# Fixed places on TensorE for the last inverse rows of a convolution, and another order of the first two gates' loads

## The chip, the cores and the metric

One core of a Trainium2 chip. The metric is device time in microseconds (us) of one launch of the whole program; lower is better. The kernel is the forward and backward pass of one layer in a single launch.

## The reference

The layer joins a long convolution (H3 style) with a bilinear gated unit; the kernel returns the output and the gradients of nine inputs. With B = 1, S = 2048, D = 1024, F = 3584, all in bf16:

```python
def ref_A(q, k, v, shift_k, ssm_k, ssm_D):
    k_shift = sum(k_pad[:, t:t + S, :] * shift_k[:, ks - 1 - t] for t in range(ks))
    kv = k_shift * v
    y = irfft(rfft(kv, 2 * S) * rfft(ssm_k, 2 * S))[:S]      # along S, per channel
    return q * (y + kv * ssm_D)

def ref_B(x, w_gate, w_up, w_down):
    h = (x @ w_gate) * (x @ w_up)
    return h @ w_down

xn = layernorm(x)
s = ref_A(xn, k, v, shift_k, ssm_k, ssm_D)
g = silu(ref_B(xn, w_gate, w_up, w_down))
out = x + s * g
# returned: out, and the gradients of x, k, v, shift_k, ssm_k, ssm_D, w_gate, w_up, w_down
```

## The kernel before

**Stages.** The 2048 rows are 16 blocks of 128 rows, the 1024 channels 8 slices of 128. First come the gate and up products (L645, 14 slabs of 256 columns), with the forward convolution running beside them on VectorE. Then come the down products `h @ w_down` (L969), taken as 8 pairs of blocks; each block has 28 chunks `fc` of 128 rows of `w_down`, and each chunk two halves of 512 columns, so a block has 56 matmuls and a pair 112. Behind each block stands a gate (`gate`, L1198): silu, its derivative, the output, and the gradients that go on. The weight gradients, the backward convolution and the last products with the layer norm's gradient follow.

**The forward convolution** is a transform along the rows, done per channel slice: short matmuls with cosine tables, and sums and differences on VectorE between them. It is a generator, `conv_forward` (L686), that yields after each piece a weight in us. `make_pump` (L465) gives two handles: `pump(frac)` takes pieces until the weights add up to that share of `F_TOTAL`, and `drain()` takes all that are left. `tick()` calls `pump` after each group of products, in the first pair after each odd chunk, so that the convolution's pieces are traced among the products.

**The last inverse.** For the last slice `inv8` (L395) leaves 16 segments of 256 values in the tile HX (called G in the code). `tail` (L744) then makes four row pairs: `inv8_rows` (L433) runs four matmuls for a pair (two rows, two segments each) into psY, a pool with a single buffer, and ScalarE copies psY into the tile yf (L750). After the fourth the tile goes to DRAM as YFd on GpSimd's queue. Row r reads the segments 2r and 2r + 1. The additions write the segments 0, 1, 4, 5, 8, 9, 12 and 13; the last four instructions of `inv8` (L283) write the pairs (2, 15), (10, 7), (14, 3) and (6, 11) in this order.

**The first pair.** Its down products are `bm_first` (L973): for a chunk, two matmuls for block 0 and two for block 1. Their PSUM is `ps_bm`, two buffers; blocks 2, 5, 8 and so on use `ps_bx`, one buffer. `bm_first(range(fc_, NF))` at L1260 traces all chunks that are left, then `drain()` at L1261 the rest of the convolution, so that the four row pairs are traced behind the first pair's products and ahead of block 2's. Then the gates of blocks 0 and 1 are traced, each with four loads on SyncE's queue: x, the output's gradient do, xn, and its rows of y, yf, which it reads back from YFd. After that the pairs 1 to 7 follow.

**Who sets the order.** The program isn't run as traced. A scheduler puts the instructions of each engine in an order, by trace order and by when it reckons that the inputs are there. Two marks bind it: `tc.keep_in_program_order(ins)` keeps the marked instructions in trace order among themselves (VectorE's, while `PIN[0]` is set, as it is through the forward convolution), and `with tc.issue_after(ins):` queues what is traced inside, on the engine of `ins`, behind `ins`. On the chip each engine works its own list in order, and so does each DMA queue.

## Time and profile before

| | |
|---|---|
| median of 3 runs | 1925.8 us (1925.4 to 1925.92) |
| the profiled execution: time, span | 1923.68 us, 1921.9 us |
| TensorE busy, matmuls | 1909.1 us (99%), 10946 |
| VectorE busy | 1554.5 us (81%) |
| ScalarE busy, GpSimd busy | 638.8 us (33%), 330.9 us (17%) |
| granted TensorE clock | 1.000 |
| first pair's down products | 511.8 to 537.0 us |
| the last four row pairs on TensorE | 537.0 to 545.7 us |
| store of yf issued, first load of yf issued | 546.8 us, 552.2 us |
| VectorE's first instruction that reads yf | 555.1 us |

Times inside the profile count from the start of the span, in us. A line of the order of time has the start, the length, the engine, the source line and operation, the tile written and the tiles read, and the count of merged instructions; in brackets the idle time of that engine before it, and what ended it. Matmuls overlap, so that one of 512 columns has a length of 0.379 us while the next starts 0.216 us after it. DVE is VectorE, ACT ScalarE, POOL GpSimd, SP SyncE, PE TensorE; SPq is SyncE's DMA queue.

### The profile page before, as it was taken

To read this page: it belongs to the slowest core of one execution; us is meant where nothing else is said; L and a number is where in the kernel's file an instruction comes from. 1 tells how busy PE (TensorE), PEld (TensorE's weight loads), DVE (VectorE), ACT (ScalarE), POOL (GpSimd) and SP (SyncE) were. 2 spreads that over 40 slices of the span, in tenths; PEclk is the share of its full clock that TensorE was granted. 3 is DMA by queue.
4 is the path that set the end of the run, shared out by engine and by line. 5 is a ranking of instruction groups with operands and counts; after the bars stand their busy time and mean duration, and the time that the engine had idled before them with its cause. 6 is when DMAs were issued, how large, how long until landed. Compare 5 with 4: busy or idle time off the path is not lost.

```text
span 1921.9 us, 27410 instructions
## 1 busy us (share of the span) xinstructions
PE 1909.1 (99%) x10946; PEld 1028.1 (53%) x10946; DVE 1554.5 (81%) x1715; ACT 638.8 (33%) x943; POOL 330.9 (17%) x461
## 2 busy tenths in 40 slices
PE   8999999999999999999999999999999999999999
PEld 5555655555544456666666666664444444444444
DVE  8999999999967555887899999999996403388785
ACT  5754655545432233332222322221212102011113
POOL 5121212201112220001022131121212101011111
PEclk9999999999999999999999999999999999999999
DMA  8786867668799988657788688585796999889885
GB/s 296 266 262 217 261 208 236 219 219 279 262 272 326 304 296 249 205 190 240 244 256 269 214 261 261 196 273 174 230 251 174 154 204 215 157 184 186 176 174 188
DMA packets 451375, 444.41 MB, mean 231 GB/s; under 512 B 268816, under 2 KB 371628, under 8 KB 436784
## 3 DMA queue, kind: packets, MB, share of 16 engines
q1 hardware_dynamic: 394864, 243.36, 48.2%
q0 software_dynamic: 40064, 169.95, 27.7%
q10 hardware_dynamic: 16320, 29.36, 4.2%
q8 instruction: 85, 1.39, 0.3%
q14 instruction: 42, 0.34, 0.1%
HBM read 194.00 MB, written 185.64 MB: 198 GB/s over the span
## 4 chain that ended last, share of the span: by engine, by line
PE 71%; issue 17%; DVE 6%; POOL 3%; DMA 3%; ACT 1%; SPq 0%; POOLq 0%; DVEq 0%; ACTq 0%
PE psx L1472 20%; PE psb L1342 20%; PE psb L1420 9%; PE psb L1325 9%; PE psg L645 8%; PE psF L235 2%; DVE W L213 1%; DMA A<-DYd 1%; POOL Hd L66 1%; PE psY L1128 1%; PE psY L438 1%; PE psx L1420 1%; DVE HX L213 1%; DVE KX L213 1%; DMA yf_t<-YFd 1%
## 5 line engine op out<-in xcount | busy, mean ns | idle before, releaser
L645 PE MATMUL psg<-wslab,U 128*128 128x512 bf16 x1792 | 407.7, 379 | 2.9 <-DMA wslab<-in_B_w_gate_dram 2.0
L1342 PE MATMUL psb<-U,U 128*128 128x512 bf16 x1792 | 397.1, 379 | 0.0
L1472 PE MATMUL psx<-U,dgut 128*128 128x512 bf16 x1536 | 332.8, 379 | 0.0
L1472 PEld LDWEIGHTS <-dgut 128*128 128x128 bf16 x1792 | 175.3, 98 | 211.4
L1342 PEld LDWEIGHTS <-U 128*128 128x128 bf16 x1792 | 175.3, 98 | 197.9
L645 PEld LDWEIGHTS <-U 128*128 128x128 bf16 x1792 | 172.5, 98 | 187.5 <-issue 2.6
L1325 PE MATMUL psb<-wdt,U 128*128 128x256 bf16 x1792 | 205.6, 273 | 0.0
L1325 PEld LDWEIGHTS <-U 128*128 128x128 bf16 x1792 | 175.2, 98 | 29.2
L213 DVE TENSOR_TENSOR W<-W 128x1024 f32<-128x1024 f32 (+1 forms) x186 | 183.9, 1005 | 3.9
L1420 PE MATMUL psb<-U,U 128*128 128x512 bf16 x816 | 177.1, 379 | 0.0
L1347 ACT CAST wb<-psb 128x512 bf16<-128x512 f32 x112 | 65.6, 586 | 315.4 <-PE psb L1342 304.4
L969 PE MATMUL psbm<-U,ht 128*128 128x512 bf16 x672 | 145.7, 379 | 0.0
L1420 PEld LDWEIGHTS <-U 128*128 128x128 bf16 x896 | 87.5, 98 | 104.5
L647 ACT CAST gut<-psg 128x512 bf16<-128x512 f32 x156 | 91.5, 588 | 123.6 <-PE psg L645 122.8
L1504 ACT ACTIVATE dx_t<-dxn 128x1024 bf16<-128x1024 f32 x15 | 15.9, 1057 | 319.4 <-DVE dxn L213 319.4
L1180 DVE SCALAR_TENSOR_TENSOR dkp<-dkT,kT 128x1024 bf16<-128x1024 bf16 (+2 forms) x64 | 78.3, 1224 | 37.6 <-DMA dkT<-DKSHd 35.9
L969 PEld LDWEIGHTS <-ht 128*128 128x128 bf16 x672 | 65.6, 98 | 78.6
L213 DVE TENSOR_TENSOR U<-U,dht 128x2048 bf16<-128x2048 bf16 x56 | 68.3, 1221 | 47.1 <-ACT dht L1327 47.1
L1327 ACT CAST dht<-psb 128x512 bf16<-128x512 f32 x112 | 65.7, 587 | 116.3 <-PE psb L1325 116.3
L66 POOL DMA_DIRECT2D Hd<-hN x54 | 37.0, 686 | 280.2 <-DVE hN L213 278.0
L213 DVE TENSOR_TENSOR dxn<-psx,dxna_t 128x1024 f32<-128x1024 f32 x15 | 18.3, 1222 | 76.5 <-PE psx L1472 70.7
L1451 ACT CAST wbs<-psb 128x512 bf16<-128x512 f32 x51 | 29.9, 586 | 145.3 <-PE psb L1420 137.2
(237 smaller groups left out, 2447.5 us busy)
## 6 DMA issues: line engine op xcount, KB each, us to landing
U<-GUd SPq DMA_DIRECT2D x28, 1024.0 KB, 7.5
DGd<-U SPq DMA_DIRECT2D x28, 1024.0 KB, 5.9
GUd<-gut ACTq DMA_DIRECT2D x39, 512.0 KB, 6.5
out_dram<-wb SPq DMA_DIRECT2D x112, 128.0 KB, 4.0
U<-Hd SPq DMA_DIRECT2D x14, 1024.0 KB, 6.0
Hd<-hN POOLq DMA_DIRECT2D x54, 256.0 KB, 4.7
HTd<-hT SPq DMA_DIRECT2D x52, 256.0 KB, 3.9
ht<-HTd SPq DMA_DIRECT2D x6, 1536.0 KB, 10.5
```

The source lines that it names most:

```text
L66: ins = nc.gpsimd.dma_start(out=out, in_=in_)
L213: pinned(V.tensor_tensor(o, a, b, op))
L645: gu_mm[0] = nc.tensor.matmul(ps[:], XNT[q][:, dc, qi * P:(qi + 1) * P], w[:, dc].rearrange("p a f -> p (a f)"), start=(dc == 0), stop=(dc ...
L647: nc.scalar.copy(out=gut[:, :, i], in_=ps[:].rearrange("p (a f) -> p a f", a=2))
L969: mm = nc.tensor.matmul(ps[:, dh * 512:(dh + 1) * 512], ht(fc)[:, i * P:(i + 1) * P], WD[fc // 4][:, fc % 4, dh * 512:(dh + 1) * 512], sta ...
L1180: ins = V.scalar_tensor_tensor(prod[:].rearrange("p r d -> p (r d)")[:, lo:H], dkT[:, 0, lo:H], 1.0, kT[:, 0, 13 + m + lo:13 + m + H], op0 ...
L1325: nc.tensor.matmul(ps[:, x * SLW:(x + 1) * SLW], DBMT[2 * hf + g][:, dc, (b % 4) * P:(b % 4 + 1) * P], wdt[:, dc, :], start=(dc == 0), sto ...
L1327: nc.scalar.copy(out=dht[:, 2 * e:2 * e + 2].rearrange("p b f -> p (b f)"), in_=ps[:])
L1342: nc.tensor.matmul(ps[:], XN[b // 4][:, b % 4, dc * P:(dc + 1) * P], dgus[b // 8][:, :, b % 8], start=(b == 0), stop=(b == NB - 1))
L1347: nc.scalar.copy(out=wb[:, dc % 2].rearrange("p a f -> p (a f)"), in_=ps[:])
L1420: nc.tensor.matmul(ps, h[:, f, b, :], DBM[b // 4][:, b % 4, dh * 512:(dh + 1) * 512], start=(b == 0), stop=(b == NB - 1))
L1472: nc.tensor.matmul(ps[:, dh * 512:(dh + 1) * 512], t[n][:, f, i * P:(i + 1) * P], WGU[n][:, f, dh * 512:(dh + 1) * 512], start=(n == 0 and ...
```

## The change

It has two parts.

The generator's piece ahead of the last four row pairs yields 1e6 in place of 3.0, so that `pump` stops there, and a third handle, `step()`, takes exactly one piece. The first pair's products are traced up to chunk 22, `pump(1.0)` traces what is left of the convolution up to that stop, and then each `step()` traces one row pair. Each row pair is queued behind the products traced just before it, and the products after it are queued behind its last matmul: chunk 23, row pair 0, chunks 24 and 25, row pair 1, chunks 26 and 27, row pair 2, chunks 0 to 2 of block 2, row pair 3, the other chunks of block 2.

The loads of a gate become a function of their own, `gate_rows`. For blocks 0 and 1 the loads of x, do and xn of both are traced first, then the loads of yf of both, and they are no longer queued behind the last weight load.

```diff
+    inv_mm = [None]
+
     def inv8_rows(G, psp, rp):
...
-                nc.tensor.matmul(ps[:, i, :], TI[:, 0, r, k, :], G[:, 2 * r + k, :], start=(k == 0), stop=(k == 1))
+                inv_mm[0] = nc.tensor.matmul(ps[:, i, :], TI[:, 0, r, k, :], G[:, 2 * r + k, :], start=(k == 0), stop=(k == 1))
...
+        def step():
+            next(gen, None)
+
...
-        yield 3.0
+        yield 1e6
         for _ in tl:
             yield 1.0
...
+    rows_in = {}
+
+    def gate_rows(b, first=0, last=None):
+        c, r = divmod(b, 8)
+        ins = []
+        for nm_, src in (("x_t", xq[:, c, r, :]), ("do_t", gout[:, c, r, :]), ("xn_t", xnn[:, c, r, :]), ("yf_t", YFd[:, b, :]))[first:last]:
+            t = mi.tile([P, D], BF16, name=nm_)
+            ld(t[:], src)
+            ins.append(t[:])
+        return ins
+
     def gate(b, ps):
         c, r = divmod(b, 8)
-        ins = []
-        for nm_, src in (("x_t", xq[:, c, r, :]), ("do_t", gout[:, c, r, :]), ("xn_t", xnn[:, c, r, :]), ("yf_t", YFd[:, b, :])):
-            t = mi.tile([P, D], BF16, name=nm_)
-            with tc.issue_after(wd_ld.ins) if b < 2 else nullcontext():
-                ld(t[:], src)
-            ins.append(t[:])
+        ins = rows_in.pop(b) if b in rows_in else gate_rows(b)
...
-    bm_first(range(fc_, NF))
+    bm_first(range(fc_, 23))
+    pump(1.0)
+    for fcs in ((23,), (24, 25), (26, 27)):
+        with tc.issue_after(inv_mm[0].ins):
+            mm = bm_first(fcs)
+        with tc.issue_after(mm.ins):
+            step()
+    ps2 = ps_bx.tile([P, D], F32, name="psbm")
+    with tc.issue_after(inv_mm[0].ins):
+        for fc in range(3):
+            mm = bm_mm(ps2, ht1[0], 0, fc)
+    with tc.issue_after(mm.ins):
+        step()
     drain()
...
+    for i in range(2):
+        rows_in[i] = gate_rows(i, 0, -1)
+    for i in range(2):
+        rows_in[i] += gate_rows(i, -1)
     for i in range(2):
         gate(i, pss[i])
...
-            ps = (ps_bx if (2 * bp + i) % 3 == 2 else ps_bm).tile([P, D], F32, name="psbm")
-            for fc in range(NF):
-                bm_mm(ps, ht, i, fc)
+            first = 2 * bp + i == 2
+            ps = ps2 if first else (ps_bx if (2 * bp + i) % 3 == 2 else ps_bm).tile([P, D], F32, name="psbm")
+            for fc in range(3 if first else 0, NF):
+                with tc.issue_after(inv_mm[0].ins) if first else nullcontext():
+                    bm_mm(ps, ht, i, fc)
```

More of the change, by code (lines that the diff above doesn't have):

```diff
@@ L481, in drain @@
             return n
-        return pump, drain
+        return pump, drain, step
     def staggered(main, tail, lag):
@@ L914, in build_kernel @@
     ps_cv = pool("ps_cv", 2, space=PSUM)
-    pump, drain = make_pump(conv, F_TOTAL)
+    pump, drain, step = make_pump(conv, F_TOTAL)
     cnt = [-5]
@@ L1190, in build_kernel @@
     C_TOTAL = 11.0 + 8 * FWD8_W + 16 * (PROD_W + INV8_W) + 8 * 1.4 + 8 * 2.5
-    bpump, bdrain = make_pump(conv_backward(), C_TOTAL)
+    bpump, bdrain, _ = make_pump(conv_backward(), C_TOTAL)
     ddo = const.tile([P, 8], BF16, name="ddo")
@@ L1465, in build_kernel @@
     PIN[0] = True
-    kpump, kdrain = make_pump(dk_units(kw_), DK_TOTAL)
+    kpump, kdrain, _ = make_pump(dk_units(kw_), DK_TOTAL)
     kcnt = [0]
```

## The prediction

> **What bounds the kernel now.** I read the waits of TensorE first, then the busy times by stretch, then the order of time on TensorE and VectorE around the edited place. TensorE is busy for 1909.1 of 1921.9 us. After the first 40 us it waits once for another engine; the columns are the total in us, the number of times and the longest:

> ```profile
> PE psY L438 <- DVE HX L283: 2.5, 1, 2.5
> ```

> That is the second row of the last inverse transform (TensorE at L438) waiting for VectorE. The stretches around it (length, then busy us of TensorE, its weight loads, VectorE, ScalarE, GpSimd, each with a count, then granted clock, DMA share and GB/s):

> ```profile
> 300.00:537.00 237.00, 236.60 (x1431) 129.18 (x1429) 234.63 (x227) 123.97 (x175) 34.23 (x48) 1.00 0.75 247
> 537.00:546.00 9.00, 6.46 (x38) 3.56 (x37) 5.18 (x8) 1.82 (x4) 0.00 (x0) 1.00 0.69 165
> ...
> 760.00:1300.00 540.00, 540.00 (x3421) 331.88 (x3420) 492.46 (x484) 155.99 (x260) 87.04 (x115) 1.00 0.74 238
> ```

> Two things matter. From 300 to 537 us VectorE is busy 99% of the time, so the moment at which it ends the last inverse is fixed by its own work. And from 546 us on TensorE has next to no gap (213.88 of 214.00, then 540.00 of 540.00), so whatever TensorE loses at the edited place nothing later gives back. Here is TensorE's order of time (start, length, line, operation, count, and the idle time before it):

> ```profile
> 517.38 19.80 PE L969 MATMUL psbm<-U,U 128*128 128x512 bf16 x91
> 537.02 0.38 PE L438 MATMUL psY<-HX,TI 128*128 128x256 bf16 x2
> 537.24 0.81 PE L969 MATMUL psbm<-U,U 128*128 128x512 bf16 x3
> 540.52 0.27 PE L438 MATMUL psY<-HX,TI 128*128 128x256 bf16 x1 [2.47 <-DVE HX L283]
> 540.63 1.02 PE L969 MATMUL psbm<-U,U 128*128 128x512 bf16 x4
> 541.73 0.27 PE L438 MATMUL psY<-HX,TI 128*128 128x256 bf16 x1
> 541.84 1.02 PE L969 MATMUL psbm<-U,U 128*128 128x512 bf16 x4
> ...
> 545.30 0.60 PE L438 MATMUL psY<-HX,TI 128*128 128x256 bf16 x4
> ```

> And VectorE's:

> ```profile
> 531.08 2.49 DVE L213 TENSOR_TENSOR HX<-W 128x512 bf16<-128x512 f32 x4
> 533.61 2.29 DVE L213 TENSOR_TENSOR W<-KX 128x2048 f32<-128x2048 bf16 x1
> 535.93 3.81 DVE L213 TENSOR_TENSOR W<-W 128x1024 f32<-128x1024 f32 x4
> 539.78 2.50 DVE L283 SCALAR_TENSOR_TENSOR HX<-W 128x512 bf16<-128x512 f32 x4
> 549.84 0.69 DVE L213 TENSOR_TENSOR gg<-bm,sig 128x1024 bf16<-128x1024 bf16 x1 [7.56 <-ACT sig L1212]
> ```

> The product loop gives 112 products to the first pair (28 chunks, 2 blocks, 2 halves). The trace has 16 from 511.78, 5 from 515.68 and these 91, so the first pair's last product stands right before 537.02. Spacing: (537.02 - 517.38) / 91 = 0.216 us. The products from 537.24 on belong to block 2. Row pair 0 of the inverse is rows 0 and 1: row 0 reads segments 0 and 1 of HX, written by the additions of 531.08; row 1 reads segments 2 and 3, and these come from the first and the third of the four instructions of 539.78, which the matmuls of 540.52 and 541.73 follow at once.

> **The change part by part.** (1) *Fixed places.* The new order is: chunk 23, row pair 0, chunks 24 and 25, row pair 1, chunks 26 and 27, row pair 2, three chunks of block 2, row pair 3, the rest of block 2. Each step is queued behind the last, so TensorE can't pull products past a row that isn't ready. Adding up the weights of the forward convolution, all of VectorE's work is traced when the planned stop comes (416.8 of 422.0), so each step does release one row pair. Row pair 0 thus moves 16 products ahead of where it stands now: chunk 23 ends at 517.38 + 75 x 0.216 = 533.6 us. Its first row goes at once (2 x 0.11 us, to 533.8), its second waits for VectorE. That engine has no gap in which to be earlier, and nothing of it is removed, so the matmuls come at 540.52 and 541.73 as now. At 541.84 TensorE has 96 products behind it; now it has 112 + 4 + 4 = 120 (one of the four after 537.24 is missing from the records). It is 24 products behind: **24 x 0.216 = 5.2 us**. Seen by gaps: 6.7 us idle in place of 2.5, and no four products between 540.63 and 541.73. After that no row waits: row pair 1 stands 8 products (1.7 us) later, at 543.6, and needs row pair 0's copy out of the single buffer, which ends at 542.6 (ScalarE, 0.59 us from 542.03), and segments from 539.78, the last done at 542.3. The next two have 1.7 and 1.3 us of products as their cover; without it each would cost about 0.9 us (0.3 to the copy's start, 0.59 for it).

> (2) *The clock after the gap.* A gap of 6.7 us, with one matmul and another 1.1 us behind it, is not in the trace before. The nearest rows are on both sides. The gap of 2.47 us is followed by products at full speed: four in 1.02 us, (1.02 - 0.38) / 3 = 0.21 us apart. The start of the program, where TensorE comes from rest, is not:

> ```profile
> 1.42 6.00 PE L521 MATMUL tr<-ident 128*128 128x128 bf16 x58 [1.42 <-POOL ident masks.py:199]
> 7.26 0.61 PE L586 MATMUL tr<-ident,x 128*128 128x128 bf16 x8
> ```

> 58 small matmuls take 5.84 us to the next, 0.101 us each; the eight after them start 0.056 us apart (7.26 to 7.71). The slow start cost 58 x 0.045 = 2.6 us. So the price is between 0 and 2.6 us, and no gain is possible since the products run at full speed now. I take **2.6 us**, since 6.7 us is nearly three times the gap that was harmless. The granted clock reads 1.00 at the start too, so that column won't tell. [...]

> (3) *Rows of the gates.* The eight loads of the first two gates stay on SyncE's queue, in another order: x, do and xn of both blocks, then both yf. Now the first yf holds the queue until the store of yf has landed, with the second block's four behind it:

> ```profile
> 547.09 0.33 SPq L61 DMA_DIRECT2D xn_t<-XNd  x1
> 552.24 0.33 SPq L61 DMA_DIRECT2D yf_t<-YFd  x1
> 552.62 0.43 SPq L61 DMA_DIRECT2D x_t<-in_A_q_dram  x1
> ```

> Six loads of about 0.4 us now fit into that wait, so the second block's come 4 us earlier. Worth for the end: nothing. VectorE works without a gap from 555.08 to 566.85 and so reaches the second gate when the first is through. TensorE needs from the gates only free PSUM: block 3 starts at about 553.5 and its buffer is copied out by 547.4; block 5 starts at about 578 and its buffer by 562.4. That cover of 6 and 16 us grows, since TensorE is later. The dropped ordering behind the last weight load (SyncE, 524.90) has no effect: these loads wait for the room of HX, and the first goes at 545.93, right behind the last row.

> (4) *What is late next.* Row pair 3 ends at 547.9 instead of 545.7, or 550.5 with the slow clock, so the store of yf and the gates come 2 to 5 us later: less than TensorE's own delay, so they set nothing.

> **Sum.** 5.2 + 2.6 = 7.8 us on the profiled execution's own 1923.7 us (span 1921.9 and 1.8 around it): 1931.5. The median of the runs is 2.1 us above that execution, so on it: 1925.8 + 7.8 = **1933.6 us**.

> **The rivals.**
> A, the forecast: 6.7 us gap and a slow restart, 1933.6. Chance 0.66.
> B, the gap without the slow restart: 1925.8 + 5.2 = 1931.0. For it: the 2.47 us gap did no harm. Against it: the start did. 0.15.
> C, not slower: the last four instructions of 539.78 are through by 533.6, because all of VectorE's work is now traced ahead of chunk 23. Then both waits vanish, 2.5 us and the 0.35 us of weight-load gaps, and the time is 1925.8 - 2.8 = 1923.0. It decides from the point where VectorE ends 8 us earlier; a VectorE without gaps since 300 us speaks against it. 0.08.
> D, the change doesn't do what it says: the rows are released later than their places (a step that spends itself on a piece of the transform), and end where they are now: 1925.8. The sum of weights speaks against it. 0.03.
> E, a second wait further on: all that follows is placed anew, and VectorE is 91% busy from 760 to 1300, so one row or product could come to wait as long as this one did: 1933.6 + 2.5 = 1936.1. For it only that tightness; against it, not one such wait now. 0.08.

> **Numbers.** A's own range is 1931.8 to 1935.2. The range of 8 in 10 takes in B below and ends short of E above: **1930.4 to 1936.0**. It leaves out C, D and most of E. A measurement here can't tell less than 0.2%, 3.9 us, from no change. A, B and E are beyond it, slower: 0.89. C and D are within it: 0.10. Faster by over 3.9 us would need more idle time than TensorE has at this place: 0.01.

> **What would show it.** The wait of L438 for HX at 6.7 us in place of 2.5, beginning near 533.8; 16 products after it before row pair 2; the products from 541.8 about 0.4 us apart for some microseconds (A) or 0.216 (B); rows 1 to 3 without a wait; the second gate's x, do and xn issued ahead of yf; TensorE without a gap thereafter. I am wrong if VectorE ends HX before 539, if products of block 2 stand ahead of row pair 0, or if TensorE gains a gap after 560.

## The result and the profile after

The changed kernel takes 1932.97 us (median of 8 runs, 1930.67 to 1941.11), the kernel before on the same chip 1925.53 us (8 runs, 1924.04 to 1927.16). The ratio is 1.0045, with a 95% interval of 1.0029 to 1.0062: slower by 7.4 us in the medians. The profiled execution took 1941.11 us, its span is 1939.3 us: the longest of the eight, and it has a second loss that the other profile of this kernel doesn't have, as the experiments show.

The waits of TensorE in the kernel after, past the first 20 us (total in us, times, longest):

```profile
PE psY L440 <- DVE HX L283: 7.4, 2, 6.6
PE psx L1501 <- DMA dgut<-DGd: 6.9, 2, 3.8
```

The first is the wait of before, tripled. The second is new and lies 1100 us later. TensorE's order of time at the edited place:

```profile
517.12 16.14 PE L974 MATMUL psbm<-U,U 128*128 128x512 bf16 x73
533.31 0.38 PE L440 MATMUL psY<-HX,TI 128*128 128x256 bf16 x2
540.28 0.37 PE L440 MATMUL psY<-HX,TI 128*128 128x256 bf16 x1 [6.59 <-DVE HX L283]
541.48 0.37 PE L440 MATMUL psY<-HX,TI 128*128 128x256 bf16 x1 [0.83 <-DVE HX L283]
541.65 3.62 PE L974 MATMUL psbm<-U,U 128*128 128x512 bf16 x8
545.06 1.06 PE L440 MATMUL psY<-HX,TI 128*128 128x256 bf16 x4
545.91 2.17 PE L974 MATMUL psbm<-U,U 128*128 128x512 bf16 x8
...
549.65 0.60 PE L440 MATMUL psY<-HX,TI 128*128 128x256 bf16 x4
550.09 23.04 PE L974 MATMUL psbm<-U,U 128*128 128x512 bf16 x104
```

Row pair 0 now comes 16 products earlier, and its second row waits until VectorE has written the segments that it reads: it starts at 540.28, against 540.52 before. The eight products from 541.65 take 3.41 us to the next line, 0.43 us each; the eight from 545.91 take 2.01, all but the first two at 0.22. The products ran at half pace for about five microseconds. VectorE's last inverse has not moved; only the first gate behind it comes 4 us later:

```profile
535.69 3.81 DVE L213 TENSOR_TENSOR W<-W 128x1024 f32<-128x1024 f32 x4
539.53 2.50 DVE L283 SCALAR_TENSOR_TENSOR HX<-W 128x512 bf16<-128x512 f32 x4
554.19 0.69 DVE L213 TENSOR_TENSOR gg<-bm,sig 128x1024 bf16<-128x1024 bf16 x1 [12.16 <-ACT sig L1223]
```

The stretches (length, busy us of TensorE, its weight loads, VectorE, ScalarE, GpSimd, then granted clock, DMA share, GB/s) show the half pace as a clock of 0.70 over 17 us, and no loss from 760 to 1300 us:

```profile
533.00:550.00 17.00, 9.53 (x40) 4.43 (x39) 8.86 (x10) 1.75 (x3) 0.00 (x0) 0.70 0.80 193
...
760.00:1300.00 540.00, 539.94 (x3443) 334.03 (x3442) 492.39 (x487) 159.88 (x264) 86.81 (x115) 1.00 0.73 235
...
1520.00:1910.00 390.00, 381.27 (x1726) 172.54 (x1760) 221.30 (x314) 50.67 (x72) 54.80 (x91) 0.99 0.94 190
```

In stretches of a quarter of a microsecond the clock reads 0.50 from 536.24 to 546.47 us, 10.24 us in all: it was halved while TensorE still waited, 2.5 us after its last matmul had ended (533.69), and stayed so for 6.2 us behind the wait.

On SyncE's queue the second gate's loads (551.82 to 552.76) do stand ahead of both loads of yf:

```profile
551.82 0.42 SPq L61 DMA_DIRECT2D x_t<-in_A_q_dram  x1
...
558.44 0.91 SPq L61 DMA_DIRECT2D yf_t<-YFd  x2
```

For comparing executions, call the **place time** the span from the last product of chunk 23 until the first pair, 20 products of block 2 and the four row pairs are through. Its work is 36 x 0.216 + 16 x 0.109 = 9.5 us. Before it was 545.74 - 533.57 = 12.2 us; after, with 14 more products added at 0.216 us since the rows end with 6: 550.09 + 3.02 - 533.31 = 19.8 us.

### The profile page after: what moved, and what is told of

It is laid out like the page before. It is cut to its first block, busy times and chain, and to the rows that moved or that the text cites. A ratio compares the mean times of both kernels' runs of the same rounds, so it can differ in the third digit from the quotient of the medians.

```text
span 1939.3 us, 27276 instructions
## 1 busy us (share of the span) xinstructions
PE 1907.9 (98%) x10812; PEld 1029.3 (53%) x10946; DVE 1554.3 (80%) x1715; ACT 638.5 (33%) x943; POOL 329.7 (17%) x461
## 4 chain that ended last, share of the span: by engine, by line
PE 83%; DVE 8%; DMA 4%; issue 2%; ACT 2%; SPq 1%; DVEq 0%; POOL 0%; ACTq 0%; POOLq 0%
PE psb L1371 20%; PE psg L650 18%; PE psb L1354 10%; PE psx L1501 9%; PE psb L1449 9%; PE psbm L974 9%; PE psF L235 3%; DVE dkp L1185 2%; DMA dkT<-DKSHd 2%; PE tr L679 1%; PE psY L440 1%; DMA dgut<-DGd 1%; DVE dxn L213 1%; DVE W L213 1%; PE psY L1133 1%
## 5 line engine op out<-in xcount | busy, mean ns | idle before, releaser
L650 PE MATMUL psg<-wslab,U 128*128 128x512 bf16 x1734 | 401.8, 379 | 5.2 <-DMA wslab<-in_B_w_gate_dram 1.1
L213 DVE TENSOR_TENSOR W<-W 128x1024 f32<-128x1024 f32 (+1 forms) x186 | 183.9, 1005 | 3.9
L213 DVE TENSOR_TENSOR U<-U,dht 128x2048 bf16<-128x2048 bf16 x56 | 68.2, 1220 | 45.9 <-ACT dht L1356 45.9
L213 DVE TENSOR_TENSOR dxn<-psx,dxna_t 128x1024 f32<-128x1024 f32 x15 | 18.3, 1222 | 82.7 <-PE psx L1501 77.4
```

The lines of the kernel that those rows point to most:

```text
L213: pinned(V.tensor_tensor(o, a, b, op))
L650: gu_mm[0] = nc.tensor.matmul(ps[:], XNT[q][:, dc, qi * P:(qi + 1) * P], w[:, dc].rearrange("p a f -> p (a f)"), start=(dc == 0), stop=(dc ...
```

## The experiments

Each was timed in rounds with the kernel before on the same chip. Runs of the first group share a kernel before of 1924.99 us (30 runs), the second 1925.05 (29), the third 1924.99 (23).

**The changed kernel once more.** No edit.

> The changed kernel once more, for a second profile of it. Theory A (an idle gap of 6.6 us makes the array run slowly afterwards): the profile again has a gap of 6.5 to 6.8 us ahead of row 1, and products about 0.43 us apart from 541.7 us on for 3 to 6 us; the time up to the end of the edited place is 6.5 to 8.5 us behind the kernel before. The second thing to see is the last stage: the first profile has two waits of TensorE for transposed loads (6.9 us) near 1660 us. If these come with the shift of the work, they stand here again; if they are chance of an execution, they are gone or elsewhere, and the time is then near 1931.

1931.34 us (9 runs, 1930.04 to 1939.02), ratio 1.0035 (1.0022 to 1.0048). The gap is 6.59 us again, products 0.43 us apart follow, the place time is 19.2 us. The wait near 1660 us is gone; this execution (1939.02 us) has another one instead, the transposes of a late gate at 720 us:

```profile
PE tr L1244 <- DVE dbm L213: 6.0, 1, 6.0
```

So the place loses nearly the same in both executions, and each late wait stands in one execution only. From 596 us on VectorE, ScalarE, GpSimd and SyncE have their instructions in the order of before.

**The fixed places alone**, with the gates' loads in the order of before and behind the last weight load again:

```diff
-    for i in range(2):
-        rows_in[i] = gate_rows(i, 0, -1)
-    for i in range(2):
-        rows_in[i] += gate_rows(i, -1)
```

> The fixed places alone, the loads of the gates as before. Theory A (the whole loss is TensorE's wait and the slow restart): as the whole change, 5 to 8 us over the kernel before. Rival (the loads matter, by moving the gates' work and DMA traffic): less than half of that.

1930.78 us (10 runs), ratio 1.0029 (1.0019 to 1.0039), a gap of 6.58 us, a place time of 20.1 us. The rows are the loss.

**The loads' order alone**, with the first pair and the rows traced as before:

```diff
-    bm_first(range(fc_, 23))
-    pump(1.0)
...
+    bm_first(range(fc_, NF))
     drain()
```

> The order of the loads alone, the rows as the scheduler put them. Theory A: no change, within 1 us of the kernel before, TensorE's wait 2.5 us as before. Rival (the loads matter): 2 us or more to either side.

1925.92 us (12 runs), ratio 1.0002 (0.9993 to 1.0011), 0.9 us over the kernel before in the medians. No change, as theory A has it. Its profile held a surprise, since TensorE's order here is that of before: the gap of 2.76 us was followed by slow products, four of them 0.43 us apart from 542.10 on, and the place time is 14.1 us.

**The gap filled with work.** 36 products more, ahead of row pair 0:

```diff
+        if fcs == (23,):
+            with tc.issue_after(mm.ins):
+                for _ in range(36):
+                    mm = nc.tensor.matmul(ps2[:, 0:512], HT0[0][:, 0, 0:P], WD[0][:, 0, 0:512], start=True, stop=True)
         with tc.issue_after(mm.ins):
             step()
```

> The whole change, and 36 products of 0.216 us (7.8 us, results overwritten later) between chunk 23 and row pair 0, so that TensorE works where it would wait for VectorE. The order of the kept work and its due time at row 1 stay. Theory A (5.2 us of wait plus a slow restart of about 2.4 us): the products after 541.7 us are 0.216 us apart, no slow stretch, and the time is 5.2 us over the kernel before, about 1930.7, so 1 to 3 us under the changed kernel. Rival B (the slow restart costs nothing for the end, the wait is all): the same time as the changed kernel within 0.5 us.

1929.13 us (12 runs, 1928.57 to 1933.64), ratio 1.0022 (1.0012 to 1.0031). Its order of time:

```profile
535.03 7.93 PE L1280 MATMUL psbm<-U,U 128*128 128x512 bf16 x36
542.80 0.60 PE L440 MATMUL psY<-HX,TI 128*128 128x256 bf16 x4
543.24 1.89 PE L974 MATMUL psbm<-U,U 128*128 128x512 bf16 x8
```

No wait, products 0.216 us apart (1.73 us for eight), a place time of 549.30 + 3.02 - 535.03 = 17.3 us. It does 36 products more than the changed kernel and is 2.2 us faster. That is the price of the slow restart; B falls. The 36 products were sized to the wait, so the 17.3 us are the 9.5 of the bare work and 7.8 of filling; what the run adds is that no product behind them is slow. Against the kernel before it is 4.1 us slower, where 5.2 was expected; the next run suggests why.

**The kernel before once more.** No edit.

> The kernel before once more, for a second profile and for the spread of equal kernels: a ratio of 1 within its interval. [...] Rival (a gap of this length is always harmless, or always harmful): as in its first profile, products 0.216 us apart after the gap.

1925.15 us (12 runs), ratio 0.9994 (0.998 to 1.0007). The wait is 2.47 us as in the first profile, but what follows differs, against the rival:

```profile
540.32 0.27 PE L438 MATMUL psY<-HX,TI 128*128 128x256 bf16 x1 [2.47 <-DVE HX L283]
540.43 1.02 PE L969 MATMUL psbm<-U,U 128*128 128x512 bf16 x4
541.52 0.27 PE L438 MATMUL psY<-HX,TI 128*128 128x256 bf16 x1
541.63 1.66 PE L969 MATMUL psbm<-U,U 128*128 128x512 bf16 x4
543.08 1.06 PE L438 MATMUL psY<-HX,TI 128*128 128x256 bf16 x4
543.94 1.70 PE L969 MATMUL psbm<-U,U 128*128 128x512 bf16 x4
```

The products are at full pace at first, then slow down. The clock, in the same stretch as in the profile after:

```profile
533.00:550.00 17.00, 14.46 (x67) 6.91 (x66) 8.90 (x10) 4.33 (x6) 1.14 (x1) 0.90 0.76 188
```

In quarters of a microsecond it reads 0.50 from 541.87 to 545.29 us, 3.41 us in all; in the first profile it reads 1.00 throughout. The place time is 13.8 us, 1.7 more than in the first profile. So the kernel before pays for a slow restart in some executions too: in two of the three profiles with its order of TensorE, by 1.7 and 2.0 us. About 1 us on average would bring the filled gap's 5.1 us (17.3 - 12.2) to the 4.1 measured.

The timed executions bear this out. Each has its mean granted clock on record, to three digits, and 3.41 us at half clock lower the mean of 1922 us by 0.0009. Of the 94 executions of the kernel before (the three groups and this repeat) 36 read 1.000, with a median of 1923.98 us, and 48 read 0.999, with 1925.10. With executions of 1.000 alone, in the first group, the filled gap (11 runs, 1928.98) stands 4.9 us over the kernel before (10 runs, 1924.09). This sorts the runs after the event, so it is a check, not a test of its own.

**A part of the gap filled**, with 12 products in place of 36 (one execution):

> The whole change with 12 products (2.6 us, results overwritten later) between chunk 23 and row pair 0 in place of 36, so that about 4 us of the gap are left. The end of the place stays, since VectorE sets it. Theory A (any gap long enough sets off a slow stretch of the same length): products from 541.7 us on about 0.43 us apart for 3 to 5 us, as with the gap of 6.6 us. Rival (the slow stretch grows with the gap): a stretch of about half that length.

```profile
540.70 0.27 PE L440 MATMUL psY<-HX,TI 128*128 128x256 bf16 x1 [3.85 <-DVE HX L283]
541.90 0.37 PE L440 MATMUL psY<-HX,TI 128*128 128x256 bf16 x1 [0.94 <-DVE HX L283]
542.07 3.44 PE L974 MATMUL psbm<-U,U 128*128 128x512 bf16 x8
545.35 0.60 PE L440 MATMUL psY<-HX,TI 128*128 128x256 bf16 x4
545.78 1.89 PE L974 MATMUL psbm<-U,U 128*128 128x512 bf16 x8
```

1930.39 us. The eight products take 3.28 us, the next eight are at full pace; the place time is 18.8 us, 1.5 over that of the filled gap. After 6.6 us of idling the excess was 2.5, 1.9 and 2.8 us in three executions, after 3.9 us it was 1.5, after 2.5 to 2.8 us it was 0, 1.7 and 2.0. The clock reads 0.50 for 3.41 us here, as after the two short gaps that were followed by it (its mean over the 17 us from 533 is 0.90 in all three), and for 10.24, 6.83 and 10.24 us after the gaps of 6.6 (0.70, 0.80 and 0.70), part of it during the wait. So in these six profiles the stretch had one of three lengths and was not set by the gap's length alone; which of the two theories holds for the price, one execution can't say.

**The fixed places later**, twice in separate groups. The whole first pair and 13 chunks of block 2 stand ahead of row pair 0, and two chunks ahead of each of the others; loads as before:

```diff
-    bm_first(range(fc_, 23))
+    bm_first(range(fc_, NF))
     pump(1.0)
-    for fcs in ((23,), (24, 25), (26, 27)):
...
+    ps2 = ps_bx.tile([P, D], F32, name="psbm")
+    done = 0
+    for upto in (13, 15, 17, 19):
+        with tc.issue_after(inv_mm[0].ins):
+            for fc in range(done, upto):
+                mm = bm_mm(ps2, ht1[0], 0, fc)
+        done = upto
+        with tc.issue_after(mm.ins):
+            step()
     drain()
```

> The fixed places moved later, loads as before: the whole first pair and 13 chunks of block 2 (5.6 us of products) stand ahead of row pair 0, and two chunks of block 2 between the next row pairs, so that VectorE is through with HX when row pair 0 comes. Theory A (all of the loss is TensorE's idle time ahead of row 1 and what it does to the clock): no wait of TensorE for HX and no slow products; the time is 2.8 us (2.5 of wait, 0.35 of weight-load gaps) under the kernel before, and up to 1 us more if the kernel before itself now and then pays for a slow restart, so 1921 to 1922.5. Rival (the rows' lateness costs: the store of yf, the gates, block 3's PSUM): a wait of block 3's first product or later, and no gain over the kernel before.

> The kernel e5_late once more, since its twelve times were spread from 1921.2 to 1942.7 us. Theory A (its place is mended, and the spread is waits for loads that come in some executions of any kernel): most times near 1921 to 1922, 3 to 4 us under the kernel before of the same call, and the late executions have waits for loads outside the edited place. Rival (the later rows leave the gates too little room, so TensorE waits later): the median no lower than the kernel before.

The place is mended. The first execution's order of time:

```profile
527.74 15.06 PE L974 MATMUL psbm<-U,U 128*128 128x512 bf16 x69
542.63 0.60 PE L440 MATMUL psY<-HX,TI 128*128 128x256 bf16 x4
543.07 1.03 PE L974 MATMUL psbm<-U,U 128*128 128x512 bf16 x4
```

No wait and no slow product, a place time of 9.5 us: the bare work. Yet the medians are 1927.2 us (12 runs, 1921.2 to 1942.68; ratio 1.0004, 0.9984 to 1.0024) and 1928.62 us (12 runs, 1921.2 to 1933.6; ratio 1.001, 0.9993 to 1.0027). Of the 24 times 9 are under 1924 us and 14 over 1926.9. Theory A's time, 1921 to 1922.5, and its "most times near 1921 to 1922" did not come; the rival's sign, a median no lower than the kernel before, did. The second profile (span 1931.6 us) shows where one long execution lost its time. TensorE's wait, SyncE's queue, and VectorE:

```profile
PE tr L1245 <- DVE dbm L213: 8.6, 1, 8.6
```

```profile
677.42 18.51 SPq L1296 DMA_TRANSPOSE U<-DBMd  x1
696.03 0.52 SPq L61 DMA_DIRECT2D do_t<-in_grad_out_dram  x1
...
697.42 0.48 SPq L61 DMA_DIRECT2D yf_t<-YFd  x1
```

```profile
708.89 0.69 DVE L213 TENSOR_TENSOR so<-xn_t,yf_t 128x1024 bf16<-128x1024 bf16 x1 [15.57 <-DMA yf_t<-YFd]
```

A transposing load holds SyncE's queue for 18.5 us; in the two profiles of the kernel before it takes 4.9 and 5.1. The loads of a gate stand behind it, VectorE waits for its yf, and TensorE for the gate's dbm, which it turns at 714.7 us. The queue is not all of it: yf, issued at 697.42, took another 11.4 us or so to land (4.1 and 6.6 for the two of that time in the first profile of before). From 680 to 700 us the DMA engines moved 144 GB/s at a busy share of 1.24, against 251 GB/s at 0.79 before, and GpSimd's stores from 674 to 700 us landed after about 15 us (one of dbm after 16.3) in place of 5 (4.3 to 5.5 by tile in the first profile of before). So these transfers were slow there, and why is open. The first repeat of the changed kernel lost its 6.0 us in the same way, behind the same load, at 14.06 us.

**The later places with the change's order of loads**, also twice. The edit is the one above on the whole change.

> The later places of the kernel e5_late and the change's order of the gates' loads. Theory A: as e5_late within 1 us, since the loads' order changes nothing that TensorE waits for. Rival (the loads' order costs or gains): 2 us or more from e5_late.

> The kernel e6_late_loads once more. Theory A: as its first time, most times near 1921.4 us, 3 to 4 us under the kernel before, and equal to the kernel without the new order of the loads within 1 us. Rival (the loads' order is what keeps the later rows from costing): 2 us or more under e9_late_2.

1921.47 us (12 runs, 1920.48 to 1938.87; ratio 0.9989, 0.9966 to 1.0012) and 1921.15 us (12 runs, 1920.67 to 1927.63; ratio 0.9987, 0.9978 to 0.9996). Of 24 times 19 are under 1924 us, 5 over 1926.5. The second time the interval lies below 1, and the median is 3.8 us under that of the kernel before: the version that beats both. It is also 5.7 and 7.5 us under the later places without the loads' order, against theory A, which had them equal both times. The two medians fall on either side of a divide, so they make the difference look large: 14 of 24 executions were late without the loads' order and 5 of 24 with it, and the lowest times are 1921.2 against 1920.5 and 1920.7. In its two profiles the transposing load still held the queue for 9.8 and 13.3 us, with no wait of TensorE.

The gain itself is small: the ratios are 0.11% and 0.13% under 1, the first interval takes in 1, and the prediction had called anything under 0.2% no change. With executions of clock 1.000 alone it is 2.8 us the first time (1921.34 against 1924.12) and 2.6 the second (1920.96 against 1923.56), about the 2.8 that the removed wait was reckoned at.

## Why the prediction was right, point by point

**The mechanism** was right, and so was the time: 1933.6 forecast, 1932.97 measured. That 7.8 us came so near to 7.4 is in part luck: the repeat and the fixed places alone lost 6.4 and 5.8, since the kernel before pays for a slow restart itself in about half of its executions (by its mean clock), and four of the eight first times (1934.58 to 1941.11) are longer than the place explains. The wait of row 1 is 6.6 us where 6.7 was forecast, it starts at 533.5 where 533.8 stood, and the rows after it wait for nothing.

**The 5.2 us of lost products** are shown: row pair 0 is through 8.34 us after chunk 23, and TensorE has done no product in that time; before, in 8.27 us, it had done 24. With the gap filled, and no slow restart, the place time is 5.1 us over that of the first profile of before.

**The 2.6 us of the slow restart** is the right size (2.5, 1.9 and 2.8 us in three executions, 2.2 us between the timed kernels), though it was taken from the start of the program, where the slow stretch is 5.8 us long, and one of the two rows that bounded it was misread. That a gap of 2.47 us does no harm was true of one execution; the same gap cost 1.7 us in the next. So the baseline pays part of the price itself, and the change adds less than 5.2 + 2.6 wherever it does. That the granted clock wouldn't tell was wrong: it reads 0.70 over the 17 us after, and 0.90 in the same stretch of the second profile of before.

What sets the half clock off, and what ends it, was not shown. A wait of 2.47 us was followed by it in one execution of the kernel before and not in the other, and in the changed kernel's first profile the clock was halved after 2.5 us of idling, so the length of the gap alone doesn't decide.

**The loads at nothing** held for the change as made (ratio 1.0002 alone). The reasoning behind it didn't: it looked only at the first gates and at TensorE's need for free PSUM. With the later rows 5 executions of 24 were late under the new order and 14 under the old. What was left out is the other need, the turned gates of the last blocks, whose loads stand on SyncE's queue behind a transposing load. How the order of eight loads near 550 us reaches a queue at 677 us was not traced, and from 572 us on the two later kernels have the same order on VectorE, ScalarE, GpSimd and SyncE; that stays open, and with so few executions so does whether it is the loads' order at all.

**No gap of TensorE thereafter** was wrong for two profiled executions (6.9 us near 1660, 6.0 us at 720). A gap after 560 us was one of the prediction's own signs of being wrong, and by it these two count against it. Rival E had named such waits, but from VectorE between 760 and 1300 us, where there is none (539.94 of 540.00); both came with late loads. These waits come and go between executions of the same program; the kernel before has times over 1926.9 us too, 12 of 52 in the last two groups.

## What to carry to other kernels

Where one engine is full and hands its last result to another, a hand-written place is right only if it stands behind enough other work to cover the moment at which the full engine ends; count that work in products, from the trace, and put the rows after it. A short wait of TensorE can cost more than its length: a place that removes a wait of 2.5 us was worth 3.6 and 3.8 us here in the medians. And when a place is mended and the median doesn't move, look at the spread: here 14 of 24 executions came late, and in the one of them that was profiled the gain was lost to slow loads far behind the edit.
